# Two transformer blocks in one kernel: how the first loads are queued and cut, how the first tile is started, and who issues the last store

## The chip, the cores and the metric

The kernel runs on 1 core of one Trainium2 chip. The metric is the device time of one execution in microseconds (us). Its engines are named as in the profile: PE (TensorE, matrix products), ACT (ScalarE), DVE (VectorE), POOL (GpSimd) and SP (SyncE, which here only issues DMAs). The time before is 326.23 us, the median of 3 runs (325.82 to 326.75).

## What is computed

The input x has 2048 tokens of 512 features in bf16. Two blocks are applied, and then the same two again with the same weights:

```python
phi = lambda t: jnp.where(t > 0, t + 1, jnp.exp(t)) + 1e-6
# _A_ref(x, wqkv, wo): linear attention, 32 heads of 16
q, k, v = split(x @ wqkv)
pq, pk = phi(q), phi(k)
kv  = einsum("bhsd,bhse->bhde", pk, v);  z = einsum("bhsd->bhd", pk)
o   = einsum("bhqd,bhde->bhqe", pq, kv) / (einsum("bhqd,bhd->bhq", pq, z)[..., None] + 1e-6)
return o @ wo
# _B_ref: layernorm, gelu(y @ w1 + b1) @ w2 + b2, with 1792 hidden features
x = x + _A_ref(_layernorm(x), A_wqkv, A_wo)
x = x + _B_ref(_layernorm(x), B_w1, B_b1, B_w2, B_b2)
x = x + _A_ref(_layernorm(x), A_wqkv, A_wo)
x = x + _B_ref(_layernorm(x), B_w1, B_b1, B_w2, B_b2)
```

## The kernel before

**Tiles.** The 2048 tokens are 16 tiles of 128 (numbered 0 to 15), four to a chunk. Chunk c is one load of 512 KB; tile 4c+k has the rows 4p+k of the chunk, p being the partition. The chunks come in the order `C0 = (3, 0, 1, 2)`, so tiles 12 to 15 are first. The two passes are L = 0 and L = 1.

**A program from a graph.** The code first records every operation with its engine, its reads and writes, its tiles of memory and an assumed duration (`Graph.op`, line 82). A `Scheduler` (line 114) then walks five lists that are written out in `CONF["ORDER"]` (from line 345), one for each of PE, ACT, DVE, POOL and SP, and settles which buffer and which of the eight PSUM banks each tile gets. Each engine runs its list strictly in that order; semaphore waits are added wherever an operation reads what another engine or a DMA wrote, or reuses its buffer. The assumed landings of the first loads are in `LAND` (line 341, in ns). So an operation that waits holds everything behind it in its engine's list.

**The names in the lists** are the ones that the texts use: `x0`, `x1`, `x2`, `xc0` to `xc2` for loads of x; `wk0`, `wk1`, `wq` for weights; `statsA0_12`, `aggr`, `cen`, `veps`, `pow`, `ysc` for the steps of the layernorm of tile 12 in pass 0; `PTA0_12` for its transposes on PE and `tcA0_12` for the copy out of PSUM; `TA0_0` for a transpose by DMA; `K0_12` and `Q0_3_0` for the key product of tile 12 and the query product of chunk 3, first tile; `expk`, `reluk`, `mink`, `phik` for phi; `G` for the running product of phi(k) and y; `W1`, `gelu`, `W2`, `RB` (the residual addition) and `OD` (the store) for the MLP.

**The first loads** (lines 657 to 672). SP issues, in this order, the first row set of chunk 3 (`x0`, 128 KB, line 658), the second (`x1`, 128 KB), half of the key weights (`wk0`, 256 KB), the third and fourth row sets (`x2`, 256 KB, line 660), the query weights (`wq`, 512 KB, line 670) and the three other chunks (line 654). ACT issues the other half of the key weights (`wk1`, line 667) at its start. The weight matrix `A_wqkv` has 512 rows of 1536 bf16 values, queries, keys and values side by side; so a key half or the query part is read in rows of 1 KB, `x0` and `x1` in rows of 1 KB, `x2` in rows of 2 KB, and a chunk in rows of 4 KB.

**The first tiles.** PE runs matmuls on constants to begin with (`warm`, line 706: eight of 512 and four of 128 columns; `N_IDLE` gives further ones after a tile's transposes, here eight and one, line 1214). Tile 12 is normed in steps: DVE statistics and centring (lines 744, 746, 725), four PE transposes (line 807), one ACT copy (line 817), then K (line 862), whose result is multiplied by the tile's 1/std inside the exponential and the relu of phi (lines 832, 843). The statistics of tile 13 are two passes on ACT with a sum (lines 732, 739); those of the other tiles are DVE's. Its PE list begins

```python
"warm PTA0_12 idle0_0 PTA0_13 K0_12 idle0_1 K0_13 PTA0_14 Q0_3_0 Q0_3_2 G0_12_0 PTA0_15 K0_14 Q0_3_1 "
```

PSUM tiles of the transposes in pass 0 belong to a class `t0` of which two may be held at a time (line 620).

**The end.** The last tile's second product is made in two parts of 384 and 128 columns (`TAIL`, line 1169). Each part is added to x by DVE (line 1174) and stored by SP (line 1176). SP's list ends `... OD14 OD15_0 OD12 OD11 OD15_1`, PE's `... W21_9_7 W21_15_h0 W21_11_7 W21_15_h1`. After its list SP waits for the semaphores of all stores (line 1320).

Of the kernel before, what the change touches and what calls it, by code (L numbers as in the profile page):

```python
# [10 lines left out]
P = 128  # L11
S = 2048
D = 512
# [59 lines left out]
class Graph:  # L73
    def __init__(self):
        self.ops = []
        self.grp = ""
        self.writer = {}
        self.readers = {}

        self.parts = {"w1": ("w1_0", "w1_1"), "w2": ("w2_0", "w2_1"), "wk": ("wk_0", "wk_1")}  # L80
# [202 lines left out]
def assign_waits(graph, order, sems, dma_sems):  # L283
# [10 lines left out]
    while len(done) < total:  # L294
        moved = False
        for e in ENGINES:
# [43 lines left out]
    N_WARM2=4, N_IDLE=[8, 1], XQ='sp', WKQ='sp act', WK1=1,  # L340
    LAND={'x0': 3220, 'x1': 4450, 'wk1': 5200, 'wk0': 6080, 'x2': 6750, 'wq': 8250, 'xc0': 9520, 'xc1': 10800, 'xc2': 12050},
    C0=(3, 0, 1, 2), N_WARM=8, ZC=(0, 3), LQ='sp', N_HALF=1, N_K=4, N_Q=3, P_Z0=6.15, N_PB=1, N_PT=8, P_DEN=-50.43,
# [37 lines left out]
        "act":  # L380
# [164 lines left out]
def build_kernel(nc, A_x, A_wqkv, A_wo, B_x, B_w1, B_b1, B_w2, B_b2, out, conf=None, report=False):  # L545
# [5 lines left out]
    with ExitStack() as es:  # L551
# [47 lines left out]
        def bank(t, n=512):  # L599
            return ps[:, t.slot, 0:n]  # L600
# [16 lines left out]
            "g4": ((0,), 1),  # L617
            "k0": ((5, 4, 6, 7), cf["N_K"]),
            "q0": ((5, 4, 6, 7), cf["N_Q"]),
            "t0": ((7, 6, 5, 4), 2),  # L620
            "t": ((7, 6, 5, 4, 3, 2, 1, 0), 2),
            "n": ((6, 7, 5, 4, 3, 2, 1, 0), cf["N_N"]),
        })
# [20 lines left out]
        def x0ap(c, k):  # L644
            return t4[:, x0[c].slot, k * D:(k + 1) * D]
# [733 lines left out]
```

## Time and profile before

| What | Value |
|---|---|
| median of 3 runs | 326.23 us |
| the profiled execution itself | 326.32 us |
| its span, first to last instruction | 324.6 us |
| PE busy in the span | 320.2 us (99%) |
| ACT, DVE, POOL busy | 197.2, 216.6, 132.3 us |
| ACT's table loads | 14, of 1.28 us |
| DMA in the span | 20.39 MB, 63 GB/s on average |

The page gives busy time by engine, the span in 40 slices, the chain of work that ended last, and groups of instructions with their mean durations. PE's busy time holds its waiting matmuls on constants too, and its matmuls overlap in the records, so a busy PE is no measure of what it got done; for that the texts count matmuls. In the chain a DMA's share runs from its issue to its landing. A row of the timeline is: start, duration, engine, line, operation, output and input, count, and in brackets the idle time before and what ended it. Two rows of the groups, as an example of the durations that are used:

```profile
L1149 ACT ACTIVATE gT<-ps,b1c 128x512 bf16<-128x512 f32 (+1 forms) x140 | 76.9, 601 | 73.1 <-PE ps L1143 72.8
L862 PE MATMUL ps<-wqkv,t 128*128 128x512 bf16 x128 | 31.2, 379 | 0.0
```

The 379 ns of one matmul is its duration with the drain; a row of four back to back takes 0.86 us in the chain, 0.216 each.

### The profile page before, as it was taken

How to read it: one execution, taken by the hardware profiler on the slowest of the kernel's cores; microseconds unless marked ns; L12 is line 12 of the kernel's file. 1: busy time of each engine (PE TensorE's matmuls, PEld its weight loads, DVE VectorE, ACT ScalarE, POOL GpSimd, SP SyncE). 2: the span in 40 equal slices, each digit the busy share in tenths (PEclk: the TensorE clock that was granted, in tenths of full speed). 3: DMA queues.
4: the chain of work that ended last, by engine and by line, in shares of the span. 5: the costliest groups of instructions: out<-in, count | busy, mean ns of one | idle time of the engine just before them, and what ended most of it. 6: DMA issues, size and time to landing. Idle time of an engine off the chain costs nothing.

```text
span 324.6 us, 4788 instructions
## 1 busy us (share of the span) xinstructions
PE 320.2 (99%) x1729; PEld 159.6 (49%) x1729; DVE 216.6 (67%) x506; ACT 197.2 (61%) x338; POOL 132.3 (41%) x224
## 2 busy tenths in 40 slices
PE   8999999999999999999999999999999999999995
PEld 4444545675544444444444444458544444444443
DVE  5997779998876871015759999999699582100422
ACT  5999799773156137898955477689913634646200
POOL 4555646436621848000175635875602635000000
PEclk9999999999999999999999999999999999999999
DMA  7514592112320134030002200120263132200014
GB/s 234 182 40 97 170 345 103 34 34 33 81 49 18 37 76 82 1 65 2 0 16 50 51 16 2 22 60 19 42 75 65 32 63 48 68 0 2 0 65 131
DMA packets 47028, 20.39 MB, mean 63 GB/s; under 512 B 42076, under 2 KB 45532, under 8 KB 47004
## 3 DMA queue, kind: packets, MB, share of 16 engines
q1 hardware_dynamic: 45676, 15.09, 20.9%
q0 software_dynamic: 1056, 4.72, 4.2%
q8 instruction: 14, 0.23, 0.3%
q10 hardware_dynamic: 272, 0.26, 0.3%
q14 instruction: 10, 0.08, 0.1%
HBM read 8.00 MB, written 2.10 MB: 31 GB/s over the span
## 4 chain that ended last, share of the span: by engine, by line
PE 96%; DMA 2%; SPq 1%; issue 0%; DVE 0%
PE ps L1143 30%; PE ps L1182 29%; PE ps L1111 9%; PE ps L862 8%; PE ps L880 5%; PE ps L963 4%; PE ps L995 4%; PE ps L893 3%; DMA wqkv<-in_A_wqkv_dram 2%; PE ps L1169 1%; PE ps L1087 1%; PE ps L944 1%; PE ps L1018 1%; PE ps L1041 1%; PE ps L807 0%; SPq L660 0%
## 5 line engine op out<-in xcount | busy, mean ns | idle before, releaser
L1149 ACT ACTIVATE gT<-ps,b1c 128x512 bf16<-128x512 f32 (+1 forms) x140 | 76.9, 601 | 73.1 <-PE ps L1143 72.8
L1143 PE MATMUL ps<-t,w 128*128 128x512 bf16 (+1 forms) x560 | 102.1, 336 | 0.0
L1182 PE MATMUL ps<-w,gT 128*128 128x512 bf16 x434 | 98.2, 379 | 0.0
L1143 PEld LDWEIGHTS ps<-t,w 128*128 128x128 bf16 x560 | 54.5, 98 | 43.9 <-ACT t L817 0.3
L1182 PEld LDWEIGHTS ps<-w,gT 128*128 128x128 bf16 x434 | 42.5, 98 | 49.8
L759 POOL TENSOR_TENSOR rstd<-veps,neghalf 128x1 f32<-128x1 f32 x64 | 37.2, 592 | 4.7 <-DVE veps L757 2.8
L832 ACT ACTIVATE eb<-ps 128x512 bf16<-128x512 f32 x56 | 31.9, 599 | 10.6 <-PE ps L862 4.5
L1192 DVE TENSOR_TENSOR pkb<-ps,xsb 128x512 bf16<-128x512 f32 x15 | 10.1, 681 | 39.4 <-PE ps L1182 37.5
L744 DVE BATCH_NORM_STATS2 stats<-xsb 128x6 f32<-128x512 f32 x48 | 32.3, 678 | 0.3
L862 PE MATMUL ps<-wqkv,t 128*128 128x512 bf16 x128 | 31.2, 379 | 0.0
L1111 PE MATMUL ps<-gtb,t 128*128 128x512 bf16 x128 | 31.1, 379 | 0.0
L845 DVE TENSOR_SCALAR eb<-eb 128x512 bf16<-128x512 bf16 x46 | 14.7, 329 | 21.3 <-ACT eb L832 21.2
L843 ACT ACTIVATE rb<-ps 128x512 bf16<-128x512 f32 x38 | 22.3, 598 | 7.6 <-PE ps L862 4.5
L749 POOL TENSOR_SCALAR veps<-mv 128x1 f32<-128x1 f32 x32 | 8.2, 256 | 36.7 <-DVE mv L746 34.9
L779 ACT ACTIVATE yb<-xsb,nmr,rstd 128x512 bf16<-128x512 f32 x21 | 16.6, 809 | 8.9 <-POOL nmr L776 8.8
L784 DVE TENSOR_SCALAR yb<-xsb,mv,rstd 128x512 bf16<-128x512 f32 x27 | 15.2, 564 | 10.0 <-POOL rstd L759 10.0
L880 PE MATMUL ps<-wqkv,t 128*128 128x512 bf16 x80 | 20.2, 379 | 0.2 <-DMA wqkv<-in_A_wqkv_dram 0.2
L1111 PEld LDWEIGHTS ps<-gtb,t 128*128 128x128 bf16 x128 | 12.3, 98 | 14.6 <-ACT gtb L976 0.5
L862 PEld LDWEIGHTS ps<-wqkv,t 128*128 128x128 bf16 x128 | 12.2, 98 | 14.1 <-ACT t L817 0.4
L1128 POOL TENSOR_TENSOR xsb<-xsb,b2b 128x512 f32<-128x512 f32 x14 | 17.3, 1238 | 3.4 <-DVE yb L784 3.2
L1315 ACT ACT_TABLE_LOAD x13 | 16.7, 1283 | 0.2
L963 PE MATMUL ps<-pkb,yb 128*128 128x512 bf16 x64 | 15.8, 379 | 0.0
(103 smaller groups left out, 380.6 us busy)
## 6 DMA issues: line engine op xcount, KB each, us to landing
w<-in_B_w_dram POOLq DMA_DIRECT2D x4, 896.0 KB, 9.2
out_dram<-pkb SPq DMA_DIRECT2D x15, 128.0 KB, 2.1
t<-in_A_x_dram SPq DMA_DIRECT2D x3, 512.0 KB, 7.5
t<-yb SPq DMA_TRANSPOSE x56, 2.5
wqkv<-in_A_wqkv_dram SPq DMA_DIRECT2D x1, 512.0 KB, 6.0
wo<-in_A_wo_dram POOLq DMA_DIRECT2D x1, 512.0 KB, 5.0
wqkv<-in_A_wqkv_dram POOLq DMA_DIRECT2D x1, 512.0 KB, 8.7
t<-t SPq DMA_TRANSPOSE x20, 2.4
```

Source lines behind the costliest of these rows:

```text
L744: G.op("dve", lambda e: e.bn_stats(stats[:, s.slot, :], src()), 602, reads=src_keys, writes=[k + "s"], tiles=[s, *src_tiles], prio=prio, n ...
L759: G.op("pool", lambda e: e.tensor_tensor(rstd[:, s.slot:s.slot + 1], veps[:, s.slot:s.slot + 1], neghalf[:], op=ALU.pow), 530, reads=[k + ...
L832: G.op("act", lambda e: e.activation(eb[:, et.slot, :], bank(bt), ACT.Exp, scale=factor()), 569 if by else 483, reads=[src_key, *more], wr ...
L843: G.op("act", lambda e: e.activation(rb[:, rt.slot, :], bank(bt), ACT.Relu, scale=factor()), 569 if by else 478, reads=[src_key, *more], w ...
L862: ins = e.matmul(bank(b), lhsT=yTa(yT)[:, dt, k * P:(k + 1) * P], rhs=wqkv[:, dt, D:2 * D], start=(dt == 0), stop=(dt == DT - 1))
L880: ins = e.matmul(bank(b), lhsT=yTa(yT)[:, dt, k * P:(k + 1) * P], rhs=wqkv[:, dt, 0:D], start=(dt == 0), stop=(dt == DT - 1))
L963: ins = e.matmul(ps[:, gb.slot + dc, :], lhsT=yb[:, y.slot, dc * P:(dc + 1) * P], rhs=pkb[:, pk.slot, :], start=(st == FIRST), stop=(st == ...
L1111: ins = e.matmul(bank(wb), lhsT=yTa(pq)[:, kt, k * P:(k + 1) * P], rhs=gtb[:, kt, :], start=(kt == 0), stop=(kt == DT - 1))
L1128: G.op("pool" if on_pool else "dve", lambda e: e.tensor_tensor(xsb[:, st, :], xsb[:, st, :], b2b[:], op=ALU.add), 1120 if on_pool else 600 ...
L1143: ins = e.matmul(bank(b, n), lhsT=w1[:, dt, ft * P:(ft + 1) * P], rhs=yTa(yT)[:, dt, k0 * P:k1 * P], start=(dt == 0), stop=(dt == DT - 1))
L1149: G.op("act", lambda e, ft=ft, b=b, k0=k0, k1=k1, n=n: e.activation(gT[:, g.slot, ft * 512 + k0 * P:ft * 512 + k1 * P], bank(b, n), ACT.Ge ...
L1182: ins = e.matmul(bank(b), lhsT=gT[:, g.slot, ft * 512 + k * P:ft * 512 + (k + 1) * P], rhs=w2[:, ft, :], start=(ft == 0), stop=(ft == FT - 1))
```

## The change

1. All first loads are issued by SP, seven instead of nine in all: `x0` now holds the first two row sets (256 KB, rows of 2 KB); `wk0` and `wk1` each hold query and key columns of half of the 512 inputs (512 KB, rows of 2 KB); `x2` holds the other two row sets; `wq` is gone. The assumed landings are new.
2. The first tile's transposes, copy, K and Q are each cut in two halves by inputs, so that a half can run when one half of the weights is there. Tile 12's first half of Q now stands ahead of K.
3. Tile 13's statistics are DVE's (`stA0_13`), like the others'.
4. The warming matmuls are seven of 512 and nine of 128 columns, the idle ones after tile 12 two instead of eight. Three transposed tiles of class `t0` may be held instead of two.
5. The store of the last 128 columns is issued by ACT.
6. The five lists are written anew throughout, under the same rules; ACT's list now changes between its function tables two times more.

```diff
@@ CONF
-    N_WARM2=4, N_IDLE=[8, 1], XQ='sp', WKQ='sp act', WK1=1,
-    LAND={'x0': 3220, 'x1': 4450, 'wk1': 5200, 'wk0': 6080, 'x2': 6750, 'wq': 8250, 'xc0': 9520, 'xc1': 10800, 'xc2': 12050},
-    C0=(3, 0, 1, 2), N_WARM=8, ZC=(0, 3), LQ='sp', N_HALF=1, N_K=4, N_Q=3, P_Z0=6.15, N_PB=1, N_PT=8, P_DEN=-50.43,
+    N_WARM2=9, N_IDLE=[2, 1], XQ='sp', WKQ='sp sp', WK1=1, K_SPLIT=1, K_HALVES=(0, 1), X_HEAD=((0, 2), (2, 2)),
+    LAND={'x0': 3540, 'wk0': 5000, 'wk1': 6400, 'x2': 7100, 'xc0': 8400, 'xc1': 9700, 'xc2': 11000},
+    C0=(3, 0, 1, 2), N_WARM=7, ZC=(0, 3), LQ='sp', N_HALF=1, N_K=4, N_Q=3, P_Z0=6.15, N_PB=1, N_PT=8, P_DEN=-50.43,
@@ ORDER, heads and ends
 "pe":
-            "warm PTA0_12 idle0_0 PTA0_13 K0_12 idle0_1 K0_13 PTA0_14 Q0_3_0 Q0_3_2 G0_12_0 PTA0_15 K0_14 Q0_3_1 "
+            "warm PTA0_12_0 PTA0_12_1 idle0_0 Q0_3_0_0 PTA0_13 Q0_3_0 K0_12_0 idle0_1 K0_12 Q0_3_1 PTA0_14 K0_13 "
+            "PTA0_15 K0_14 G0_12_0 K0_15 Q0_3_3 Q0_3_2 G0_13_0 K0_0 PTA0_1 G0_14_0 K0_3 K0_1 G0_15_0 Z0_3 G0_0_0 K0_2 "
...
 "sp":
-            "x0 x1 wk0 x2 wq xc0 xc1 xc2 TA0_0 TA0_3 TA0_2 TA0_8 TA0_5 TA0_4 TA0_6 TA0_10 TA0_7 TA0_11 TA0_9 b2 b1 "
+            "x0 wk0 wk1 x2 xc0 xc1 xc2 TA0_0 TA0_3 TA0_2 TA0_8 TA0_5 b1 TA0_10 TA0_4 TA0_6 TA0_7 TA0_11 TA0_9 Tb1 "
...
+            "TB1_13 TB1_15 TB1_14 TB1_11 OD4 TB1_9 TB1_8 OD5 TB1_10 OD13 OD2 OD12 OD14 OD6 OD10 OD0 OD15_0 OD7 OD8 "
+            "OD3 OD9 OD11",
@@ WAY
-        "pz1_3_1": "dve", "pz1_3_2": "pool", "pz1_3_3": "pool", "stA0_13": "act", "tc_10": "act", "tc_11": "dve",
+        "pz1_3_1": "dve", "pz1_3_2": "pool", "pz1_3_3": "pool", "stA0_13": "dve", "tc_10": "act", "tc_11": "dve",
@@ the first loads
-        dma("sp", lambda e: e.dma_start(x0ap(HC, 0), rows(x_dram, HC)[:, 0, :]), [("x0", FIRST)], [x0[HC]], prio=-120, name="x0", kb=128)
-        for k, n in ((1, 1), (2, 2)):
+        for k, n in cf["X_HEAD"]:
...
-            dma(q, lambda e, h=h, n=n: e.dma_start(wqkv[:, n * h:n * h + n, D:2 * D], wsrc[:, n * h:n * h + n, D:2 * D]), [f"wk_{h}"], prio=-99,
-                name=f"wk{h}", kb=128 * n, after=[ones] if q == "act" and cf["WK1"] else ())
+            dma(q, lambda e, h=h, n=n: e.dma_start(wqkv[:, n * h:n * h + n, 0:2 * D], wsrc[:, n * h:n * h + n, 0:2 * D]), [f"wk_{h}", f"wq_{h}"], prio=-99,
+                name=f"wk{h}", kb=256 * n, after=[ones] if q == "act" and cf["WK1"] else ())
         load_chunk(cf["LQ"], C0[1], -98)
-        dma(cf["LQ"], lambda e: e.dma_start(wqkv[:, :, 0:D], wsrc[:, :, 0:D]), ["wq"], prio=-97, name="wq", kb=512)
@@ transpose_pe, first tile
+            if tag == f"A0_{FIRST}" and cf["K_SPLIT"]:
+                n = DT // len(cf["K_HALVES"])
+                bs = {h: Tile(psum, f"tp{tag}_{h}", "t0") for h in cf["K_HALVES"]}
...
+                for h in cf["K_HALVES"]:
+                    def turn(e, h=h, b=bs[h]):
+                        for d in range(n * h, n * h + n):
+                            ins = e.transpose(bank(b).bitcast(BF16)[:, d * P:(d + 1) * P], yb[:, y.slot, d * P:(d + 1) * P], idp[:])
+                        return ins
...
@@ attn_k, first tile (attn_q has the same with columns 0:D and wq)
+                    def part(e, h=h, i=i):
+                        n = DT // len(halves)
+                        for j in range(n):
+                            ins = e.matmul(bank(b), lhsT=yTa(yT)[:, n * h + j, k * P:(k + 1) * P], rhs=wqkv[:, n * h + j, D:2 * D],
+                                           start=(i == j == 0), stop=(i == len(halves) - 1 and j == n - 1))
+                        return ins
...
@@ mlp_down, last tile
-                    dma("sp", lambda e, cs=cs: e.dma_start(rows(out_dram, c)[:, k, cs], pkb[:, ot.slot, cs]), [f"od{st}_{h}"],
+                    dma("act" if h else "sp", lambda e, cs=cs: e.dma_start(rows(out_dram, c)[:, k, cs], pkb[:, ot.slot, cs]), [f"od{st}_{h}"],
```

More of the change, by code (lines that the diff above doesn't have):

```diff
@@ L619, in build_kernel @@
             "q0": ((5, 4, 6, 7), cf["N_Q"]),
-            "t0": ((7, 6, 5, 4), 2),
+            "t0": ((7, 6, 5, 4), 3),
             "t": ((7, 6, 5, 4, 3, 2, 1, 0), 2),
@@ L798, in transpose_pe, with half @@
         def transpose_pe(y, ykey, yT, k, key, prio, tag, on_act, after=()):
+            if tag == f"A0_{FIRST}" and cf["K_SPLIT"]:
+                n = DT // len(cf["K_HALVES"])
+                bs = {h: Tile(psum, f"tp{tag}_{h}", "t0") for h in cf["K_HALVES"]}
+                G.parts[key] = tuple(f"{key}_{h}" for h in cf["K_HALVES"])
+                for h in cf["K_HALVES"]:
[3 more added lines that the diff above has]
+                        return ins
+                    o = G.op("pe", turn, n * 66, reads=[ykey, f"id{P}"], writes=[f"{key}_{h}p"], tiles=[bs[h], y], prio=prio, name=f"PT{tag}_{h}",
+                             lat=MM_DRAIN, n=n)
+                for h in cf["K_HALVES"]:
+                    def half(ap, h=h):
+                        return ap.rearrange("p (d s) -> p d s", d=DT)[:, n * h:n * h + n, :]
+                    r = G.op("act", lambda e, half=half, b=bs[h]: e.activation(half(t4[:, yT.slot, :])[:, :, k * P:(k + 1) * P],
+                                                                      half(bank(b).bitcast(BF16)[:, 0:D]), ACT.Copy), 144 + 0.65 * n * P,
+                             reads=[f"{key}_{h}p"], writes=[f"{key}_{h}"], tiles=[bs[h], yT], prio=prio, name=f"tc{tag}_{h}", lat=90)
+                G.writer[key + "p"] = o
+                return r
             b = Tile(psum, f"tp{tag}", "t0" if tag[:2] == "A0" else "t")
@@ L864, in fn @@
                 return ins
-            G.op("pe", fn, 4 * MM, reads=[f"yT{L}_{st}", "wk"], writes=[f"k{L}_{st}"], tiles=[b, yT], prio=prio,
-                 name=f"K{L}_{st}", lat=MM_DRAIN, n=4, after=after)
+            if L == 0 and c == HC and k < cf["K_SPLIT"]:
+                halves = cf["K_HALVES"]
+                for i, h in enumerate(halves):
+                    def part(e, h=h, i=i):
[4 more added lines that the diff above has]
+                        return ins
+                    G.op("pe", part, DT // len(halves) * MM, reads=[f"yT{L}_{st}" + (f"_{h}" if f"yT{L}_{st}" in G.parts else ""), f"wk_{h}"] + ([f"k{L}_{st}"] if i else []), writes=[f"k{L}_{st}"],
+                         tiles=[b, yT], prio=prio, name=f"K{L}_{st}" + (f"_{i}" if i < len(halves) - 1 else ""), lat=MM_DRAIN, n=DT // len(halves), after=after)
+            else:
+                G.op("pe", fn, 4 * MM, reads=[f"yT{L}_{st}", "wk"], writes=[f"k{L}_{st}"], tiles=[b, yT], prio=prio,
+                     name=f"K{L}_{st}", lat=MM_DRAIN, n=4, after=after)
             phi(b, f"k{L}_{st}", lambda: pkb[:, pk.slot, :], f"pk{L}_{st}", [pk], prio, f"k{L}_{st}", by)
@@ L882, in fn, with part @@
                         return ins
-                    G.op("pe", fn, 4 * MM, reads=[f"yT{L}_{4 * c + k}", "wq"], writes=[f"q{L}_{c}_{k}"],
-                         tiles=[b, yT], prio=prio + 0.8 * k, name=f"Q{L}_{c}_{k}", lat=MM_DRAIN, n=4)
+                    if f"yT{L}_{4 * c + k}" in G.parts:
+                        halves = cf["K_HALVES"]
+                        n = DT // len(halves)
+                        for i, h in enumerate(halves):
+                            def part(e, h=h, i=i, k=k, b=b):
+                                for j in range(n):
+                                    ins = e.matmul(bank(b), lhsT=yTa(yT)[:, n * h + j, k * P:(k + 1) * P], rhs=wqkv[:, n * h + j, 0:D],
+                                                   start=(i == j == 0), stop=(i == len(halves) - 1 and j == n - 1))
+                                return ins
+                            G.op("pe", part, n * MM, reads=[f"yT{L}_{4 * c + k}_{h}", f"wq_{h}"] + ([f"q{L}_{c}_{k}"] if i else []),
+                                 writes=[f"q{L}_{c}_{k}"], tiles=[b, yT], prio=prio + 0.8 * k,
+                                 name=f"Q{L}_{c}_{k}" + (f"_{i}" if i < len(halves) - 1 else ""), lat=MM_DRAIN, n=n)
+                    else:
+                        G.op("pe", fn, 4 * MM, reads=[f"yT{L}_{4 * c + k}", "wq"], writes=[f"q{L}_{c}_{k}"],
+                             tiles=[b, yT], prio=prio + 0.8 * k, name=f"Q{L}_{c}_{k}", lat=MM_DRAIN, n=4)
                     phi(b, f"q{L}_{c}_{k}", lambda k=k: t4[:, pq.slot, k * D:(k + 1) * D], f"pq{L}_{c}_{k}", [pq], prio + 0.8 * k,
```

5 lines of the change are left out of this document (2 added, 3 removed), and 265 rows, old and new, of the table ORDER.

## The prediction

> **What bounds the kernel now.** I read the chain of waits first, the waits of TensorE (PE) next, then the timelines of the head and of the tail, and last the windows for DMA rates. The chain that ended last:
>
> ```profile
> PE 96%; DMA 2%; SPq 1%; issue 0%; DVE 0%
> ```
>
> PE carries 96% of the span. The list of PE's waits has two entries only: 0.8 us for the start, and 0.2 us for a DMA into `wqkv` at L880. So time can come from two places: PE's time before it becomes dense, and what follows its last matmul. The head of the chain:
>
> ```profile
> 2.69 5.97 DMA wqkv<-in_A_wqkv_dram
> 8.66 0.05 issue
> 8.71 1.90 PE ps L880 x8
> ```
>
> From 8.71 us on, every link but short tails is PE. What is behind it:
>
> ```profile
> 3.42 0.69 DVE L744 BATCH_NORM_STATS2 stats<-t 128x6 f32<-128x512 bf16 x1 [1.96 <-DMA t<-in_A_x_dram]
> 4.77 0.61 PE L807 MATMUL ps<-idp,yb 128*128 128x128 bf16 x4
> 5.42 0.60 ACT L817 ACTIVATE t<-ps 128x512 bf16<-128x512 bf16 x1 [0.73 <-PE ps L807]
> 6.12 1.03 PE L862 MATMUL ps<-wqkv,t 128*128 128x512 bf16 x4
> 6.45 0.69 DVE L744 BATCH_NORM_STATS2 stats<-t 128x6 f32<-128x512 bf16 x1 [0.38 <-DMA t<-in_A_x_dram]
> 8.71 1.90 PE L880 MATMUL ps<-wqkv,t 128*128 128x512 bf16 x8 [0.20 <-DMA wqkv<-in_A_wqkv_dram]
> ```
>
> Before 8.71 PE had done K of two tiles (0.86 each; four matmuls of 0.216) and three transposes (0.22 each): 2.38 us. Its **lost time** is 8.71 - 2.38 = 6.33 us. PE's useful matmuls are the same after the change, so a change of lost time moves the end one for one. The tail:
>
> ```profile
> 320.51 0.80 PE ps L1169 x14
> 321.30 0.02 issue
> 321.33 0.29 DVE pkb L1174
> ```
> ```profile
> 321.29 0.93 SPq L1194 DMA_DIRECT2D out_dram<-pkb  x2
> 322.27 0.45 SPq L1176 DMA_DIRECT2D out_dram<-pkb  x1
> ```
>
> The last sum stands in SBUF at 321.62, but SP is still issuing two older stores and comes to it at 322.27: 0.65 us of waiting in SP's queue.
>
> **The loads.** Issue plus time to landing gives, in the DMA view: x's first row set 3.39, the second 3.95, the key half on ACT 4.99, that on SP 5.70, x2 6.4, `wq` 8.66, x chunks 9.97, 11.2, 12.4. The price of 512 KB thus depends on its rows:
>
> ```profile
> 6.00:7.00 1.00, 1.00 (x11) 0.51 (x7) 0.62 (x2) 1.00 (x4) 0.19 (x1) 1.00 0.96 331
> 9.00:10.50 1.50, 1.50 (x9) 0.67 (x8) 1.12 (x4) 1.44 (x4) 0.59 (x1) 1.00 1.01 415
> ```
>
> (Last column GB/s.) `wq`, 1 KB rows: 331 GB/s, and 2.26 us from x2's landing to its own. x chunks, 4 KB rows: 415 GB/s, 1.25 us. x2, 2 KB rows, 256 KB: 0.72 us, so 1.44 for 512 KB. The new weight halves have query and key columns side by side, 2 KB rows; I take 1.44 each, the nearest row, with ends 1.25 and 2.26. x's pair: 3.39 plus another 128 KB at x2's rate, 0.36, so about 3.7 (ends 3.4 and 3.95). Estimated landings: x0 3.7, wk0 5.15, wk1 6.6, x2 7.3, xc0 8.55, xc1 9.8, xc2 11.05. SP issues seven loads instead of eight at some 0.45 each, far ahead of these. ACT loses one issue (0.42 at 1.49), when it is idle.
>
> [...]
>
> **PE's head, walked through.** Durations are rows above and of the same timeline. The warming matmuls (seven of 512 and nine of 128 columns, in place of eight and four, at 0.427 and 0.107: 3.95 us, now 3.84) end near 4.8, before they matter. First tile: statistics at 3.73, 0.69; then 0.03, aggregate 0.18, centring 0.35, to PE at x0 + 1.38 = 5.08. Two halves of two transposes each; the first copy starts 0.44 after (the 0.65 of the row less two cold transposes of 0.107). A half copy is not in the trace: gelu takes 0.685 for 512 and 0.473 for 256 columns, so 0.60 - 0.21 = 0.39 (ends 0.30 and 0.60). Copies end at 5.9 and 6.2. wk0 (5.15) is covered by this. Half of Q of tile 12: 5.95 to 6.38. Tile 13's statistics now run on VectorE: 0.60 more there, 1.72 less on ACT (0.63, 0.71 and two reads of 0.19). Its centring ends near 6.3, transposes at 6.38 to 6.6, copy 6.8 to 7.4. Second half of Q waits for wk1: 6.65 to 7.08. K of tile 12 in halves and an idle matmul: to 8.0. Q of tile 13: to 8.87. Then x2 decides: statistics 7.33, aggregate 8.05, the next statistics 8.15, centring 8.75 to 9.1, so transposes of tile 14 at 9.15, a wait of 0.28. Behind it, in PE's order: K13 to 10.23, transposes of 15 to 10.45, K14 (ACT's copy ends at 10.3) to 11.31, G of 12 to 12.18, K15 to 13.04. Done by then: seven groups of 0.86 and four transposes, 6.93; lost time 6.11. **Gain 0.22.** With x0 at 3.45, wk1 6.0, x2 6.6 the same walk gives 5.77, a gain of 0.56; more is barred by the copies on ACT (tile 14's not before 10.0). With one load late by `wq`'s excess (2.26 - 1.44, so wk1 7.4, x2 8.1) it gives 6.9, a loss of 0.57.
>
> **After 13 us.** The new list asks for tiles earlier: K of tile 3 at about 17.6 where it was 20.07, of tile 8 at 24.0 where it was 26.13. ACT feeds them: from the copy of tile 13 (6.61) to the start of norm 8 (21.10) it does 25 instructions, 0.58 each, without a pause; after, 24 stand in between, so norm 8 starts at 6.8 + 24 * 0.58 = 20.7. Norm (0.81) and transpose by DMA (2.5 to landing) bring it to 24.0: just in time. For tile 3 the same count (12 instructions) gives 17.1, 0.5 early. SP adds the small bias load ahead of the sixth transpose, some 0.45; SP waits for ACT and VectorE there, so this is covered, and uncovered it would cost 0.45 once. POOL's second mask step (0.85) moves behind tile 13's rstd; its next one is for a tile that lands after 8 us. Slack of 0 to 0.9 a tile: I allow 0.1 us of waits (ends 0 and 0.6).
>
> **The middle.** Two more table loads on ACT, 1.28 each. The tightest place is block 2's first MLP chunk, where two switches to Exp and back now come before its last gelu. Counted from the chunk's first matmul: ACT follows PE for 24 gelus of half width to 10.9 (24 * 0.4375 + 0.4); then four loads 5.1, two exps 1.2, four gelus 1.6, three norms 2.3: 21.1. PE needs that gelu after 28 groups (12.25), two output projections (1.72) and six half groups of the second product (9.06): 23.0. Covered; beyond 1.9 us of delay PE would wait one for one. Weight loads on POOL change order, but `wo` landed at 40.4 and is used at 51.4. Nothing taken.
>
> **The tail.** ACT is free; the last store goes out at RB + 0.05, 0.05 + 0.29 + 0.03 after PE's end, instead of 0.97: 0.61 saved, landing 1.8 after issue as now. What is late next: SP's store of tile 11, issued when its addition ends, 0.05 before PE's end, landing 2.1 later; that is 2.05 against 2.15 for ACT's store, so it does not cap the gain. The stores before it, held by tile 8's (ready 1.6 before PE's end), take three issues of 0.47 and end 0.15 before. Ends: 0.3 if ACT's queue answers later, 0.75.
>
> **Sum.** 0.22 + 0.61 - 0.1 = 0.73 from the profiled execution's 326.32 (span 324.6 and 1.7 around it): **325.6**, 0.6 below the median 326.23 of the runs. A measurement of this kernel can tell about 0.3%, 1 us, from no change; this is inside.
>
> **Rivals.**
> 1. Clean landings (x2's rate or better, the fast walk): 0.56 + 0.61 = 1.17, so 325.1. For: 415 GB/s is seen. Against: the first 1.5 us of traffic ran at 185 GB/s. 0.24.
> 2. One load late as `wq` was: -0.57 + 0.61 - 0.1, so 326.4. For: the pattern is there once in nine loads. 0.13.
> 3. Slower: both weight halves come at `wq`'s pace, because it is the slow strided matrix and not the row length that sets it. Then wk1 lands at 3.7 + 2 * 2.26 = 8.2, x2 at 8.95; Q's second half starts at 8.25, tile 14 at x2 + 1.85 = 10.8; lost time 7.75, a loss of 1.4, so 327.2, and 327.45 with x's pair at its upper end: 327.3. It decides once wk1 is later than about 7.8. Against: the key halves, same matrix, 512 KB in 1.75 us after x's second set. 0.09.
> 4. The clock. Transposes took up to 311 ns at 4.77 and 219 from 5.90: full speed came near 5.7. The change leaves PE idle at 5.5 to 5.95, where before eight idle matmuls ran (now two). If that puts off full speed to 9.1, the 12 matmuls from 5.95 cost 0.43 each until then; tile 14 moves to 10.4, loss 1.2 instead of the gain: 326.9. 0.06.
>
> [...]
>
> That the change does not do what it says is not a rival: the order of instructions shows seven loads on SP, the halves and the store on ACT.
>
> **Chances.** Forecast 0.48 (325.2 to 326.1 by itself), rivals 0.24, 0.13, 0.09, 0.06. Faster by over 0.3% (below 325.25) is rival 1 and a tenth of the forecast's cases and a little for waits counted too high: 0.30. Slower (above 327.2): rival 3 and part of 4: 0.12. Within: 0.58. Range 324.9 to 327.1.
>
> **What would show it.** Q's first half at about 5.95, its second at wk1's landing (6.6); tile 14's transposes at 9.15 with a short wait before; K15 done near 13.0; no PE wait over 0.2 later; the last store issued some 0.4 after PE's end. It is wrong if PE's waits list holds ACT or DMA entries of 0.5 and more after 13 us.

## The result, and the profile after

The changed kernel takes 331.65 us (median of 4 runs, 330.45 to 331.88) against 326.49 for the kernel before (4 runs beside it): ratio 1.0151, 95% interval 1.0118 to 1.0184. It is **slower by 5 us**; 325.6 was forecast, with a range to 327.1. The profiled execution took 331.88, its span is 330.0. The chain that ended last:

```profile
PE 85%; DVE 7%; DMA 4%; POOL 2%; issue 1%; ACT 1%; SPq 0%
```

Of 96% for PE, 85 are left; VectorE (DVE), a DMA and POOL have come into the chain. The list of PE's waits (who waits, for whom, us in all, times, longest) says where; before it held two entries, the start and 0.2 for `wqkv`. The first five of nine entries are:

```profile
PE ps L1082 <- DVE kvb L1078: 1.6, 1, 1.6
PE ps L878 <- DMA t<-yb: 1.2, 1, 1.2
PE ps L823 <- DVE yb L781: 1.2, 1, 1.2
PE ps L697 <- PEq L1405: 0.8, 1, 0.8
PE ps L1184 <- ACT gT L1190: 0.7, 1, 0.7
```

Each of these waits happens once; the fourth is the start. To place them I use the lost time of the prediction at any moment: the time less what the matmuls done by then take at full pace (0.216 for 512 columns, 0.109 for 256, 0.056 for a transpose), counted from PE's weight loads in the trace. A weight load starts up to 0.2 ahead of its matmul, so that the 6.33 of the prediction, counted from matmuls, is 6.13 here.

| Useful work done, us | 14 | 16 | 42 | 48 | 56 | 70 | 100 | 300 |
|---|---|---|---|---|---|---|---|---|
| at about (before), us | 20 | 22 | 48 | 54 | 62 | 76 | 106 | 306 |
| lost, before | 6.13 | 6.13 | 6.19 | 6.19 | 6.31 | 6.23 | 6.22 | 6.23 |
| lost, changed | 5.89 | 7.32 | 7.38 | 9.12 | 11.08 | 11.81 | 11.80 | 11.83 |

Four steps: 1.4 at 21 us, 1.75 at 52, 1.95 at 62 to 65, 0.7 at 72. Ahead of them the change is 0.24 better, and behind them nothing more is lost, in spite of the two added table loads and of new lists to the end. 11.83 - 6.23 = 5.60 is the whole difference of the two profiled executions (331.88 - 326.32 = 5.56), but for the 0.1 that the tail gains.

**The head** is as forecast. Its timeline, against the rows of before:

```profile
3.53 0.69 DVE L741 BATCH_NORM_STATS2 stats<-t 128x6 f32<-128x512 bf16 x1 [2.08 <-DMA t<-in_A_x_dram]
5.65 0.60 PE L917 MATMUL ps<-wqkv,t 128*128 128x512 bf16 x2 [0.25 <-ACT t L811]
6.73 0.59 PE L917 MATMUL ps<-wqkv,t 128*128 128x512 bf16 x2 [0.24 <-DMA wqkv<-in_A_wqkv_dram]
9.09 0.40 PE L823 MATMUL ps<-idp,yb 128*128 128x128 bf16 x4
```

Q's halves start at 5.65 and 6.73 (forecast 5.95, 6.65), tile 14's transposes at 9.09 (9.15).

**At 21 us** K of tile 2 waits for its transpose by DMA. In the chain:

```profile
17.81 4.90 DMA t<-yb
```

4.90 us from issue to landing, where the median of this line's transposes is 2.5. In the DMA view of 17 to 23 us stands, beside SP's own queue, the fetch of instructions (packets, MB, share):

```profile
q8 instruction: 1, 0.02, 2.0%
```

This one packet of 16 KB starts at 19.70 and takes 1.94 us on one of the 16 DMA engines. The transpose's first engine reports at 21.06, 15 of them by 21.22, the last at 22.71. In the run `four` below, with a fetch in the same place, 15 engines report at 20.39 to 20.55, the usual 2.3 to 2.4 after the issue, and the last at 22.15: one engine's lateness sets the landing. (Why the 15 are 0.8 late here is not shown.) In the kernel before the same fetch (18.60, 1.18 us) began when the transpose, issued at 16.30, was 0.12 from its landing.

**At 52 us:**

```profile
50.58 0.78 POOL L681 DMA_DIRECT2D w<-in_B_w_dram  x1
51.03 2.79 DVE L852 TENSOR_SCALAR eb<-eb 128x512 bf16<-128x512 bf16 x1
51.38 2.29 POOL L1136 TENSOR_TENSOR t<-t,lr 128x512 bf16<-128x512 bf16 x2
53.75 0.87 DVE L1078 TENSOR_TENSOR kvb<-ps,bdmask 128x128 bf16<-128x128 f32 x4
54.08 0.39 PE L1082 MATMUL ps<-wo,kvb 128*128 128x512 bf16 x1 [1.57 <-DVE kvb L1078]
```

The minimum at 51.03 (`minq0_2_0`) normally takes 0.28. Here it takes 2.79 and ends with POOL's two products. The four `kvm` products behind it in VectorE's list come out late, and PE's M0 waits 1.57. Ahead of POOL's products stands the issue of `w1_1`, which the new list has moved there. In the kernel before, the same minimum was over 0.03 ahead of the same products:

```profile
50.06 0.28 DVE L836 TENSOR_SCALAR eb<-eb 128x512 bf16<-128x512 bf16 x1
50.37 2.40 POOL L1095 TENSOR_TENSOR t<-t,lr 128x512 bf16<-128x512 bf16 x2 [0.78 <-ACT lr L1091]
```

**At 62 us** the same happens again:

```profile
61.93 1.02 POOL L681 DMA_DIRECT2D w<-in_B_w_dram  x1
62.08 2.35 DVE L781 TENSOR_SCALAR yb<-xsb,mv,rstd 128x512 bf16<-128x512 f32 x1
62.97 1.16 POOL L1104 TENSOR_TENSOR lr<-t,zrow 128x512 f32<-128x512 bf16 x1
64.48 0.40 PE L823 MATMUL ps<-idp,yb 128*128 128x128 bf16 x4 [1.17 <-DVE yb L781]
```

The issue is that of `w2_1`, the product `pz0_3_2`; the norm takes 2.35 in place of 0.54, and PE's transposes wait for it. The load has a second effect. SP's transpose `TB0_1`, issued at 61.59, lands at 66.00, 4.41 later, while the 896 KB of `w2_1` come in (landing at 67.79); PE's first W1 begins at 66.06 and 0.25 is lost there. In the five profiles in which `w2_1` is issued beside this transpose it took 4.4 to 5.1, in the others 2.4 to 2.5.

**The tail.** The last store is ACT's, 0.34 after PE's last matmul as forecast, but SP is not done earlier:

```profile
323.62 4.12 SPq L1235 DMA_DIRECT2D out_dram<-pkb  x5
326.88 0.29 DVE L1215 TENSOR_TENSOR pkb<-ps,xsb 128x128 bf16<-128x128 f32 x1
327.20 0.40 ACTq L1217 DMA_DIRECT2D out_dram<-pkb  x1
```

Five stores in 4.12 us; the first of them took 2.16 alone. The span ends 3.19 after PE's last matmul, 3.30 before.

### The profile page after: what moved, and what is told of

It reads as the page before. It is cut to its first block, busy times and chain, and to the rows that moved or that the text cites. A ratio compares the mean times of both kernels' runs of the same rounds, so it can differ in the third digit from the quotient of the medians.

```text
span 330.0 us, 4763 instructions
## 1 busy us (share of the span) xinstructions
PE 318.6 (97%) x1696; PEld 158.2 (48%) x1727; DVE 223.6 (68%) x507; ACT 200.2 (61%) x337; POOL 133.6 (40%) x224
## 4 chain that ended last, share of the span: by engine, by line
PE 85%; DVE 7%; DMA 4%; POOL 2%; issue 1%; ACT 1%; SPq 0%
PE ps L1223 28%; PE ps L1184 28%; PE ps L878 7%; PE ps L1152 6%; PE ps L1036 4%; PE ps L934 3%; PE ps L908 3%; PE ps L1004 3%; DMA t<-in_A_x_dram 2%; DMA t<-yb 1%; DVE stats L741 1%; POOL rstd L756 1%; DVE xsb L1157 1%; PE ps L1210 1%; DVE yb L781 1%
## 5 line engine op out<-in xcount | busy, mean ns | idle before, releaser
L756 POOL TENSOR_TENSOR rstd<-veps,neghalf 128x1 f32<-128x1 f32 x64 | 39.1, 624 | 4.5 <-DVE veps L754 2.7
L878 PE MATMUL ps<-wqkv,t 128*128 128x512 bf16 x122 | 30.2, 379 | 1.3 <-DMA t<-yb 1.2
L754 POOL TENSOR_SCALAR veps<-mv 128x1 f32<-128x1 f32 x29 | 7.7, 274 | 50.5 <-DVE mv L743 46.3
L781 DVE TENSOR_SCALAR yb<-xsb,mv,rstd 128x512 bf16<-128x512 f32 x27 | 16.6, 621 | 11.2 <-POOL rstd L756 11.2
L1229 DVE TENSOR_TENSOR xsb<-ps,xsb 128x512 f32<-128x512 f32 x16 | 10.8, 678 | 17.3 <-PE ps L1223 17.3
L861 DVE TENSOR_SCALAR eb<-eb 128x512 bf16<-128x512 bf16 x46 | 14.0, 313 | 9.6 <-ACT eb L848 9.5
L746 POOL TENSOR_SCALAR veps<-mv 128x1 f32<-128x1 f32 x32 | 7.3, 229 | 31.7 <-DVE mv L743 30.2
L908 PE MATMUL ps<-wqkv,t 128*128 128x512 bf16 x74 | 18.7, 379 | 0.1
```

Of the source, the lines that this page charges most:

```text
L756: G.op("pool", lambda e: e.tensor_tensor(rstd[:, s.slot:s.slot + 1], veps[:, s.slot:s.slot + 1], neghalf[:], op=ALU.pow), 530, reads=[k + ...
L781: G.op("dve", lambda e: e.tensor_scalar(yb[:, y.slot, :], src(), stats[:, s.slot, 2:3] if by_act else mv[:, s.slot, 0:1], rstd[:, s.slot:s ...
L878: ins = e.matmul(bank(b), lhsT=yTa(yT)[:, dt, k * P:(k + 1) * P], rhs=wqkv[:, dt, D:2 * D], start=(dt == 0), stop=(dt == DT - 1))
L908: ins = e.matmul(bank(b), lhsT=yTa(yT)[:, dt, k * P:(k + 1) * P], rhs=wqkv[:, dt, 0:D], start=(dt == 0), stop=(dt == DT - 1))
```

## The experiments

Most edits move operations within the finished lists, behind the planner, so that buffers and PSUM banks stay those of the kernel that is edited. The ratios are to the kernel before on the same chip (three chips in all), where it took 326.66 to 326.82, with 95% intervals. Lost times are those of the one profiled execution.

### Four edits that tell one cause from several

Theory A held the late weight loads on POOL for the cause of the steps at 52 and 62 us; theory B held that all follow from the first, at 21 us.

**w_early.** The two late loads on POOL, `w1_1` and `w2_1`, go back among the others, ahead of `w2_0`:

```diff
-  w1_0 phik0_6 wv wo phiq0_1_2 w2_0 phiq0_1_1 pr0_0_2 w1_1 pr0_1_0 ... powB0_0 w2_1 pz0_3_2
+  w1_0 phik0_6 wv wo w1_1 w2_1 w2_0 phiq0_1_2 phiq0_1_1 pr0_0_2 pr0_1_0 ... powB0_0 pz0_3_2
```

> The changed kernel with one thing undone: the issues of w1_1 and w2_1 on POOL go back to where the kernel before has them, among the other weight loads, ahead of w2_0. Theory A (weight loads): the stalls of 1.75 us at 52 us and 1.9 us at 63 us come from these two late issues on POOL, each of which keeps a short VectorE operation waiting (2.79 us in place of 0.28, and 2.35 in place of 0.54); both go, the stall of 1.4 us at 21 us stays, and the time is 331.65 - 3.65 = 328.0, or 327.3 if the 0.7 at 72 us goes with them. Theory B (one cause): every later stall follows from the one at 21 us, which put the engines out of step; then this edit does nothing and the time stays at 331.6, within 0.5.

Measured: 329.51 us, ratio 1.0080 (1.0055 to 1.0105). The minimum now meets the end of POOL's products, not their beginning:

```profile
50.05 2.28 POOL L1136 TENSOR_TENSOR t<-t,lr 128x512 bf16<-128x512 bf16 x2
```
```profile
51.62 0.86 DVE L852 TENSOR_SCALAR eb<-eb 128x512 bf16<-128x512 bf16 x1
52.40 0.87 DVE L1078 TENSOR_TENSOR kvb<-ps,bdmask 128x128 bf16<-128x128 f32 x4
```

PE's wait for `kvb` is gone, lost time is 7.96 and 7.97 at 42 and 48. The norm at 61 us still takes 1.30, beside `pz0_3_2`, and the wait for ScalarE is 0.9. From 16 to 100 us of work 2.06 is lost in place of 4.48. Theory B is refuted. A holds for the step at 52 us whole and for 1.2 of the 1.95 at 62; the step at 72 grew from 0.7 to 1.0.

**ta2_early.** On VectorE `statsA0_2 aggrA0_2` go ahead of `minq0_3_0`, `normA0_2` goes behind `normA0_1`.

> The changed kernel with statistics and norm of tile 2 (block 0's first norm) earlier on VectorE, so that its DMA transpose is issued near 16.7 us and not at 17.81, ahead of the instruction fetch that occupies one DMA engine from 19.5 to 21.4 us. Theory A: the stall at 21 us (1.4 us) goes, those at 52 and 63 us stay: 331.65 - 1.4 = 330.2. Theory B (one cause): all stalls go, 331.65 - 5.8 = 325.9. If the late transpose has nothing to do with the fetch, its landing keeps 4.9 us after the issue and PE still waits some 0.3 to 0.5 us: 330.6 to 331.0 by A.

Measured: 332.76, ratio 1.0164 (1.0131 to 1.0197). The transpose, issued at 17.86, landed at 20.32 (2.46), ahead of the fetch at 21.13, and PE lost nothing between 14 and 16 of work (7.52, 7.54). But in this run the head had lost 7.5 and not 5.9, so no gain is to be seen in the time. The late head also moved the issue, which was to be at 16.7; with an equally late head the unedited list issues it at 19.37 (w_early). The later steps all came: B falls again.

**w_ta2** (both edits):

> Both edits in one: the two weight loads early on POOL, and tile 2's norm early on VectorE. Theory A: the gains add up, 331.65 - 3.65 - 1.4 = 326.6, or 325.9 with the stall at 72 us gone too. Theory B: 325.9, as with the norm alone. Were the lists of the rest worse for another reason (theory C), it would stay above 328.

Measured: 329.18, ratio 1.0067 (1.0045 to 1.0089), 7.65 lost by 16 and 9.65 by 70. The sum of A did not come: the head lost 1.5 more than before's, and 1.8 were still lost at 62 and 72 us.

**before_w_late** (the kernel before, `w1_1` behind `pr0_0_2`, `w2_1` behind `powB0_0`):

> The kernel before with one thing of the change: w1_1 issued on POOL behind pr0_0_2 and w2_1 behind powB0_0, where the changed kernel has them. Theory A: the same collisions appear, PE loses up to 1.75 + 1.9 us, and the time is 328 to 330; it is smaller where the VectorE operation that falls in the issue is not one that PE waits for. Theory B: nothing, 326.4.

Measured: 326.80, ratio 0.9998 (0.9988 to 1.0007). Nothing: PE's list holds no new wait behind the head. The issue of `w1_1` ends at 50.45, and the minimum (50.25, 0.30) is over when POOL's products begin (50.56). The issue of `w2_1` (59.30, 1.18) even stands beside a norm, which takes its usual 0.53 (59.45); no product of POOL follows it. So a late issue by itself held nobody here. In the changed kernel, where products follow, the minimum and the norm began 0.35 and 0.89 ahead of them, long enough to end first, and were held all the same; whether the issue has a part in that is not shown (the times of POOL's rows are rough).

### What was left of the steps

**b2_early**: as w_early, and on SP

```diff
-  TA0_9 Tb1 TB0_1 TB0_2 b2 TB0_3
+  TA0_9 b2 Tb1 TB0_1 TB0_2 TB0_3
```

> The changed kernel with the two weight loads early on POOL (as in w_early: 329.5, PE's lost time growing by 2.06 us between 23 and 80 us) and one thing more undone: the load of b2 on SP goes back behind TA0_9, so that it does not stand between the transposes TB0_2 and TB0_3. In w_early PE's queue sits 1.63 us in a wait for two transposes, until 70.92, and the second, issued behind b2 at 67.35, lands at 70.89. Theory A (b2's load holds TB0_3 back, 0.6 us on SP and 0.9 us in flight): TB0_3 is issued by 66.8 and lands by 69.4, PE's wait of 0.94 us goes, and the time is 329.5 - 0.9 = 328.6. Rival (ScalarE's 14 gelus, which end at 70.84, are the limit, as the list of waits says): nothing, 329.5.

Measured: 329.19, ratio 1.0072 (1.0051 to 1.0093); in the trace the lost time from 16 to 70 of work grew by 1.04 in place of 2.06. SP's rows of w_early and then of this run:

```profile
66.72 0.59 SPq L1273 DMA_DIRECT2D b2b<-in_B_b_dram  x1
67.35 1.19 SPq L791 DMA_TRANSPOSE t<-yb  x1
```
```profile
65.13 2.59 SPq L791 DMA_TRANSPOSE t<-yb  x2
```

The two transposes now go out back to back, and PE's wait "for ScalarE" of 0.9 is gone from its list. The list had named the wrong one: in w_early the gelus ended just ahead of the landing (70.84, 70.89).

**pz_late**: as w_early, and `pz0_3_2` on POOL behind `powB0_3`.

> The changed kernel with the two weight loads early (as in w_early) and POOL's product pz0_3_2 (1.14 us) behind powB0_3, where it does not run beside the norm of tile 0 that PE's transposes wait for. In w_early that norm took 1.30 us in place of 0.54 beside it, and PE's lost time grew by 0.45 + 0.33 us around 62 us. If VectorE waits for POOL's product: the norm takes 0.54 to 0.56, PE's transposes come at once, TB0_3 too is issued earlier by about 0.4, and the time falls by 0.6 to 1.0 from 329.5 to 328.5-328.9. If the norm is long for another reason: no change.

Measured: 328.77, ratio 1.0057 (1.0038 to 1.0076). The norm takes 0.54, the lost time is 8.23 at 48 and 8.34 at 56, so that this step is gone. (The product now meets a later norm, 1.33 at 65.03, for which PE does not wait.)

**four** (w_ta2, b2_early, pz_late together) and **four_warm** (`N_WARM2=20`):

> The changed kernel with four things put back or put right: weight loads early on POOL, tile 2's norm early on VectorE (as in w_ta2: 329.2), b2 early on SP, pz0_3_2 late on POOL. If these are what cost the time behind the first tiles, PE's lost time stays flat from 23 us on, against +1.95 us in w_ta2, and the time is 329.2 - 1.9 = 327.3; what is then left above the kernel before, some 0.5 to 1.3 us, lies in the first 12 us. If something else in the lists costs time, it stays above 328.

> The four edits, and 20 short idle matmuls in place of 9 ahead of the first tile's transposes. In the three runs before of the changed head, x's first pair landed at 4.3 to 4.5 us and not at 3.5; TensorE stood idle 0.8 to 1.2 us ahead of the transposes, and its matmuls kept 427 ns (in place of 216) until 9.1 to 9.5 us. Theory: the gap is what puts the fast matmuls off; 11 more idle matmuls (1.2 us at the slow pace, 0.6 at the fast one) cover it, the fast pace comes by 5.8 us, and the head loses 5.9 to 6.4 us in place of 7.5. With the transpose of tile 2 early nothing of that is given back at 21 us, and the time is 327.3 - 1.3 = 326.0. Rival: the fast pace comes at a time that has nothing to do with the gap, and the 11 matmuls change nothing (327.3) or put the first transposes off by up to 0.6 (327.9).

Measured: four 328.42, ratio 1.0050 (1.0032 to 1.0068); four_warm 328.13, 1.0040 (1.0024 to 1.0056). In four the lost time is 7.80 at 16 and 8.06 at 70: flat, as expected. Then it grows to 8.82 by 100, because SP's transposes now stand back to back from 80 to 89 us and PE waits 0.2 several times. What is left beside that is the head, 7.78 against 5.7 to 6.8 in six profiles with before's. In four_warm the head lost 6.54, and the matmuls were fast from 5.0 us on; a fetch at 221.9 then met a transpose that landed 4.26 after its issue, and PE lost 1.2 there. The trace is as the theory on the idle gap has it, the expected 326.0 did not come. One profile shows little here, as half of those with nine idle matmuls were fast early too (see below).

### The two halves of the change

**lists_only**: the kernel before up to 18 us as planned, the new order behind it. **head_tail**: the new head up to 14 us, the old order behind it, ScalarE's last store. **head_warm**: the same with 20 idle matmuls. Here the planner laid out buffers anew.

> The other half: the kernel before up to 18 us as planned, with its loads and its last store on SP; behind that every engine follows the changed kernel's order. Theory (the order of the rest costs the time): the collision of the late weight load with VectorE's minimum (1.75 us), that of the next with the norm (1.9), and the wait for TB0_3 behind b2's load (0.7 to 1.0) come back, PE's lost time grows by 4.0 to 4.6 us between 50 and 75 us, and the time is 326.8 + 4.3 = 331.1. The transpose of tile 2 keeps the early place of the kernel before, so the 1.4 us at 21 us do not show. Rival (the head sets the phase in which these meet): under 328.

> The change without its new lists: its loads, its halves of the first tile, its idle matmuls and its last store by ScalarE, with its order up to 14 us as planned; behind that every engine follows the order of the kernel before. If the lists of the rest are what made the changed kernel slow, PE's lost time is flat from 14 us on as before (6.1 to 6.3), and only the head and the end differ: with the head of the profiled run (0.22 less lost) and an end of 2.5 to 2.9 us behind PE's last matmul in place of 3.3 to 3.7, 326.8 - 0.2 - 0.7 = 325.9; with the heads of the last seven runs (6.5 to 7.8 lost, against 6.1 to 6.3), 326.0 to 327.7. If the loads themselves are at fault for the rest, 328 and more.

> head_tail with 20 short idle matmuls in place of 9 ahead of the first tile's transposes. In the four edits the same step took the head's lost time from 7.8 to 6.5 in the profiled runs. Theory (x's first pair lands at 4.1 to 4.5 us and the gap in front of the transposes puts the fast matmuls off until 9 us in some runs): the slowest executions of head_tail go, the time is 326.0 to 326.5 and its spread is smaller. Rival: no difference to head_tail.

Measured: lists_only 332.10, ratio 1.0165 (1.0151 to 1.0179). 6.05 lost by 14 of work, 12.18 by 100, with the same 2.79 and 2.35 us of VectorE beside `w1_1` and `w2_1`. Of these 6.1, 4.3 lie between 42 and 70 of work, as expected; 1.8 come earlier, at the seam of the two orders (21 to 25 us) and at 35. The order behind the head is enough to make the kernel slow. head_tail took 333.29, ratio 1.0208 (1.0190 to 1.0227), head_warm 333.71, 1.0214 (1.0200 to 1.0228). Neither collision is in them, but others are: 2.1 at the seam (19 to 21 us) and 3.6 between 59 and 78 us. So they do not isolate the head, and what it would cost under well-fitted lists stays open.

### The head, and one operation moved

**after_again**: the changed kernel itself, on the chip of these experiments.

> The changed kernel once more, on the chip of these runs. In its first profile x's first pair landed at 3.5 us, TensorE's matmuls were fast from 3.8 us on, and the head lost 5.9 us, followed by 1.4 us at 21 us. In the seven edits of it, whose first 12 us are the same program, the pair landed at 4.1 to 4.5 us and the head lost 6.5 to 7.8 us. If that is what executions differ in, this profile shows a late pair and 6.5 to 7.8 us lost by 14 us, less or none of the wait at 21 us, and the same time of 331 to 332.

Measured: 334.01, ratio 1.0228 (1.0212 to 1.0244). x's pair landed at 4.00 and 7.5 was lost by 14 of work, 0.1 at 21 us. As expected, but for the time, which is 2 us worse than in the first runs (the intervals do not meet). The profiled execution took 332.38; the four others took 333.63 to 334.26, and where they lost the rest no trace shows. So what an edit gains in time, by the 331.65, is known to about 2 us only; the lost times within one profile are the better measure.

**min_late**: `minq0_2_0` on VectorE behind the four `kvm0` products.

> The changed kernel with one VectorE operation moved: the minimum minq0_2_0 goes behind the four products kvm0_0 to kvm0_3 that PE's M0 waits for. The late weight loads stay. Theory: the minimum, held 2.79 us while POOL works through the load's issue and two products, is what makes the kvm products late; behind them it holds nobody up, they read PSUM and run in 0.2 each beside POOL, PE's wait of 1.6 us at 52 us goes, and the time is 331.7 (334.0 in the last run of the same kernel) less 1.6. Rival: the kvm products too wait for POOL, or the load itself delays them; then PE waits as long as before.

Measured: 332.20, ratio 1.0169 (1.0150 to 1.0188). The load is late, the issue and the products stand where they stood:

```profile
53.21 2.29 POOL L1136 TENSOR_TENSOR t<-t,lr 128x512 bf16<-128x512 bf16 x2
53.52 0.88 DVE L1078 TENSOR_TENSOR kvb<-ps,bdmask 128x128 bf16<-128x128 f32 x4 [0.57 <-PE ps L1059]
54.33 1.33 DVE L852 TENSOR_SCALAR eb<-eb 128x512 bf16<-128x512 bf16 x1
```

The `kvm` products, which read PSUM, run at their usual pace beside POOL (0.88); the minimum is held until POOL ends, and PE's wait at M0 is gone (9.2 lost at 42 and still at 47 of work). So that wait came from the held VectorE operation and what stands behind it, not from the load's data. But the loss is only moved. The late minimum makes VectorE's next operations late, and PE loses 0.5 at 57 and 0.5 at 63 us; at 68 us it loses 0.9 for `TB0_1`, which beside `w2_1` lands 5.06 after its issue. By 60 of work 3.6 have been lost since 42, against 3.7 in the changed kernel and 4.2 in after_again. In the changed kernel the minimum began ahead of POOL's products (51.03 against 51.38 and 52.50) and was held through both (2.79, to 53.82); by what, no row shows.

**x_single** and **x_single_warm**: `four` and `four_warm` with `X_HEAD=((0, 1), (1, 1), (2, 2))`, SP's list `x0 x1 wk0 wk1 x2`.

> The four edits (328.4), with x's first pair loaded as two single tiles, as in the kernel before: x0, x1, then the two weight halves and x's second pair. Theory (the pair is too large to land first): x0 lands at 3.4 to 4.1 and not at 4.0 to 4.5, the first transposes start 0.4 to 0.6 earlier, the weight halves 0.1 to 0.4 later; the head loses 6.2 to 7.0 in place of 7.8, and the time is 327.6 to 328.2. Rival (one of the 16 engines is late whatever the size): x0 lands at 4.0 to 4.5 all the same, the head loses as much or more, 328.4 to 328.9.

> x_single with 20 short idle matmuls in place of 9. If the gap ahead of the transposes is what leaves the matmuls at 427 ns until 9 us in some executions, the fast pace comes by 6.3 us in this profile, the head loses 6.2 to 6.6, and the time is 0.2 to 0.5 below that of x_single with a smaller spread. Rival: the transposes, which could start at 4.9 to 5.5, wait for the longer row of idle matmuls (to 5.9 at the slow pace), and nothing is gained.

Measured: 328.03, ratio 1.0042 (1.0027 to 1.0056), and 329.32, 1.0080 (1.0067 to 1.0093). x0 landed at 3.28 and 3.24, the transposes could start at 4.73, but the first half of the weights landed at 6.77 and 6.84 and PE waited 1.3 for it in x_single. 8.1 and 7.4 lost by 14 of work: in these two profiles the weights give back what the smaller load wins. (That of x_single is its slowest execution, 329.03; the others took 327.9 to 328.1.) With 20 idle matmuls the fast pace came at 6.2 in place of 10.1, but a fetch at 222.7 met a transpose again, issued at 220.8, which took 4.18.

### The tail

**before_act_store**: the kernel before with the change's fifth point alone.

> The kernel before with one thing of the change: the last store is issued by ScalarE and not by SP. In the three profiles with before's tail the end came 3.0 to 3.7 us behind PE's last matmul, in the eight with the changed kernel's tail 2.5 to 3.3 (mean 2.8). Theory: the term of 0.61 holds, SP's queue then ends one store earlier; 326.7 - 0.3 to 0.7 = 326.0 to 326.4. Rival: SP's slow store (1.4 to 2.2 us in nearly every run) sets the end in both, and it gives 0.0 to 0.2.

Measured: 326.56, ratio 0.9996 (0.9986 to 1.0007): no gain; the interval leaves at most 0.5 us for the 0.61. In its profile, of the slowest of twelve executions (327.74), one of SP's stores takes 2.17, and the end comes 4.00 behind PE.

**sorted_stores** and **shared_stores**, the kernel before with

```diff
-  OD2 ... OD0 ... OD4 OD1 OD10 OD5 OD13 OD7 OD9 OD6 OD3 OD8 OD14 OD15_0 OD12 OD11 OD15_1     (all on SP)
+  OD1 ... OD2 ... OD0 OD3 OD5 OD7 OD4 OD6 OD14 OD13 OD12 OD10 OD8 OD9 OD15_0 OD11            (OD15_1 on ACT)
+  shared_stores: OD6 OD14 OD13 OD10 OD8 OD9 OD15_1 on ACT
```

> The kernel before with its stores on SP in the order in which VectorE's last sums come (OD1 OD2 OD0 OD3 OD5 OD7 OD4 OD6 OD14 OD13 OD12 OD10 OD8 OD9 OD15_0 OD11), and the last one issued by ScalarE. Theory (SP's queue of nine late stores, with the slow issue among them, sets the end): only OD9, OD15_0 and OD11 are issued in SP's last 5 us, the end comes 2.4 to 2.7 us behind PE's last matmul in place of 3.3 to 4.0, and the time is 326.7 - 0.7 to 1.1 = 325.6 to 326.0: faster than both kernels. Rival (the landing of the last bytes, whoever issues them, is the end): 3.0 and more, 326.4 to 326.7.

> sorted_stores with six more stores (OD6 OD14 OD13 OD10 OD8 OD9) issued by ScalarE, which has no other work after 306.5 us. SP then issues 97 DMAs; in the profiles so far the last 16 KB fetch came when SP had issued 97 or 98. Theory (the fetch goes with SP's place in its program and lengthens the issue at that moment): no slow issue in the last 10 us, the end at 2.4 to 2.6 us behind PE's last matmul, 325.6 to 325.9. Rival (the fetch belongs to another engine or to a time): a slow issue of 1.4 to 2.2 us is there all the same, on SP or on ScalarE.

Measured: 325.43, ratio **0.9963** (0.9950 to 0.9976), and 325.30, **0.9959** (0.9945 to 0.9973). Both are faster than the kernel before, by 1.2 to 1.5 us, and so than the changed one. The end of shared_stores:

```profile
320.82 0.33 SPq L1194 DMA_DIRECT2D out_dram<-pkb  x1
320.88 0.29 DVE L1174 TENSOR_TENSOR pkb<-ps,xsb 128x128 bf16<-128x128 f32 x1
321.20 0.34 ACTq L1176 DMA_DIRECT2D out_dram<-pkb  x1
```

Each store goes out as its sum is made, in 0.33; the end is 2.56 and 2.58 behind PE, against 3.30 to 4.00 in three profiles with before's order. The fetch comes all the same (318.80 and 318.39), when SP has issued 101 and 95 DMAs, so it does not go with SP's count; it only meets no issue any more. Whose program it carries stays open.

## Why the prediction was wrong

**The loads and PE's head: right in the profiled run, not in most.** Landings were within 0.2 of the forecast, the gain was 0.24 for 0.22. This was luck: in nine more profiles with the same loads and nine idle matmuls x's pair landed at 4.0 to 4.5, wk1 at 7.1 to 7.8 (3.5 and 6.6 in the first), and 6.7 to 7.8 was lost by 10 of work. The head of the kernel before lost 5.7 to 6.8 in six profiles. In most profiles the new head is thus the slower one, by about 1 us; that is rivals 2 and 4 together, for which 0.19 was allowed. In five of the ten profiles and in x_single the matmuls stayed at 0.427 until 9 to 10 us; with 20 idle matmuls (three profiles) and with before's head (six) in none. Why x's pair lands late in some executions was not settled.

**"After 13 us ... I allow 0.1 us of waits": failed.** Tiles 3 and 8 were walked through, tile 2 was not: its transpose went from 16.30 to 17.81 while K of it was asked for sooner. Even so 17.81 + 2.5 is 20.3, in time for 21.3; the 1.4 us are the fetch's. The time in which a transpose lands was taken for a constant. Over all 20 profiles tile 2's landed in 2.41 to 2.46 where no 16 KB fetch began more than 0.15 us before the landing (ten), and in 3.5 to 4.9 where one did (ten).

**"The middle ... Nothing taken": failed, and this is the main error.** The step asked only whether a weight would arrive in time. It did; what cost 1.75 and 1.95 us is where POOL's issue and the products behind it stand, what VectorE does meanwhile, and who queues behind that; 0.25 of the 1.95 is the load's traffic beside a transpose. `b2` on SP between two transposes was not looked at; it cost 0.7, and 1.0 in w_early. With the 1.4 ahead of them these terms are 5.8 us where the prediction had 0.1. The table loads, which the step did work out, cost nothing, as said.

**The tail's 0.61: wrong.** Alone it gave 0.04% (interval across nothing). The step took SP's older stores to end 0.15 before PE, at 0.47 for each issue. In the changed kernel one of them, OD7, took 2.16 while a fetch was under way (323.74), so that SP's last store went out 0.46 after PE's last matmul and not 0.05 before it; in the trace that the step read one issue took 1.46. Before's order, of before_act_store, has OD9 ahead of four finished stores, which puts nine issues in the last 5 us.

**The rivals.** The third, both weight halves at `wq`'s pace, did not come; the second half alone took 2.2 to 2.4 in two profiles. The fourth's 9.1 us for full speed stands in no row of before; the runs showed 0.427 until 9 to 10 us in six profiles, and what sets that time was not shown. None had the engines meeting behind the head. The sentence that was to show the forecast wrong (PE waits of 0.5 and more after 13 us for ACT or a DMA) did so, with 1.2 for a DMA and 0.7; the largest wait, 1.6, was for VectorE, which it did not name.

**What the 5 us are.** Shown by taking them away, in lost time: 2.4 for the two late weight issues, 0.9 for `pz0_3_2`, 1.0 for `b2`, together 4.3 of the 4.5 lost between 16 and 70 of work (in four, 0.8 of it comes back by 100 as waits for transposes). The rest is the head with or without the fetch at 21 us: in nine profiles of the changed kernel and its edits 7.2 to 9.2 was lost by 16 of work, in five profiles of before's lists 5.7 to 6.8. Only the fetch's part of that is understood. The run four is still 1.6 us slower than the kernel before: 1.7 at the head and 0.7 between 70 and 100 of work, less 0.8 at the end. Why after_again is 2 us slower than the first runs stays open.

## What to carry to other kernels

When a list is rewritten, walk every operation that it moves on POOL and SP past the operations of the other engines at that time: a 0.8 us issue cost 1.75 us where POOL's products behind it fell on a short VectorE operation with PE's operands queued behind it. In the kernel before the two missed each other by 0.03 us. Moving one operation more can just move the loss (min_late). An in-order queue of stores wants the order in which their data are made; with the last store on ACT that was worth 1.2 us here, five times what the change tried to win at the head. A wait in the profile that lies within 0.1 us of a DMA's landing may be the DMA's.

## What the runs showed of the hardware that was not expected

- A fetch of instructions, `q8 instruction` in the DMA view, was a packet of 16 KB on one of the 16 engines, 0.9 to 2.4 us long; there were 14, 0.23 MB in all, in each of the profiles of the kernel before, the changed kernel and shared_stores. Tile 2's transpose by DMA, where it was in flight then, landed in 3.5 to 4.9 us and not in 2.4; a store being issued took 1.4 to 2.2 and not 0.45.
- `b2`'s load ahead of a transpose on the same queue raised the transpose's landing from 2.5 to 3.5 us. An 896 KB load issued by GpSimd beside a transpose raised it from 2.4 to 4.4 and more (five profiles).
- With nine idle matmuls TensorE waited 0.4 to 1.2 us ahead of the first transposes; in five of these ten profiles the matmuls stayed at half pace (0.427 us for 512 columns) until 9 to 10 us, in five they were fast already when it began or right behind it. In x_single the gap, 1.3 us, came behind the transposes, and half pace lasted as long. With before's head it did not last so long in any of six profiles, with waits of up to 1.1 us there.
